# Program order on three engines in the attention of a routing-attention and MLP kernel, and a copy moved from VectorE to ScalarE

## The chip, the cores and the metric

The kernel runs on one core of a Trainium2 chip. The metric is the device time of one execution in microseconds (us). The engines are TensorE (PE in the profile; PEld is its weight load), VectorE (DVE), ScalarE (ACT), GpSimd (POOL) and SyncE (SP), which here issues nearly all DMAs. Each engine works through its own queue, and engines wait for one another by semaphores.

## What is computed

Attention in which a query sees only the keys that fall to the same one of 16 clusters, and then an MLP block with a residual:

```python
q_assign = np.argmax(np.einsum('bhsd,hcd->bhsc', q_n, c_n), axis=-1)   # q_n, k_n, c_n: rows scaled to length 1
k_assign = np.argmax(np.einsum('bhsd,hcd->bhsc', k_n, c_n), axis=-1)
mask = q_assign[:, :, :, None] == k_assign[:, :, None, :]
scores = np.where(mask, scale * np.matmul(q, k.transpose(0, 1, 3, 2)), -1e9)
attn = softmax(scores)                     # written out in the reference, with 1e-9 in the denominator
x = (attn @ v) brought from (B,H,S,D) to (B, S, H*D)
xn = (x - mean(x)) / sqrt(var(x) + 1e-6) * g_ln
out = x + np.maximum(xn @ w_ch1, 0.0) @ w_ch2
```

B = 4, H = 8, S = 768, D = 64; the MLP goes from 512 to 2048 and back. The two weight matrices arrive as 64-bit floats, and the kernel converts them to 32 bits on VectorE.

## The kernel before

The attention runs over 16 head pairs `n` (4 batches by 4 pairs of heads). A pair has 12 steps: two halves of the queries by six blocks of 128 keys. A step is `scores` (four matmuls for two heads: two with the one-hot clusters, L317, two with q and k, L322; then one exponential of 128x768 on ScalarE, L327, into one of five buffers `e`) and `weigh` (the matmuls with v, L337, and on VectorE the addition of the exponentials into `es`, L348 or L351; after the sixth step a ScalarE copy into `xT`, L354).

The loop over `u` has six slots per pair, two steps in each. `scores` runs two steps ahead of `weigh`. Between them stands the preparation of the coming pairs and the end of the pair before:

- slot 0: `prep_transpose(n + 1, 1)`, six PE transposes of k (L230) and two copies out of PSUM, the first half by ScalarE (L236), the second by VectorE (L238);
- slot 1: `prep_sims(n + 1)`, similarities to the centroids (L247) and a ScalarE copy (L256); `finish(n - 1, 0)`, denominators by matmuls with ones (L367), a copy (L372) and four DMAs of it;
- slot 2: `prep_route(n + 1)`, three transposes (L263) and a chain of six VectorE operations (L270 to L282) that gives the one-hot clusters;
- slot 3: `finish(n - 1, 1)`, VectorE's reciprocal (L376) and two kinds of DMA, out to memory and back as a broadcast `rb`;
- slot 4: `prep_onehot(n + 1)`, twelve transposes (L295) and two ScalarE copies (L301);
- slot 5: `prep_transpose(n + 2, 0)`, the same for q; `finish(n - 1, 2)`, VectorE's scaling of `xT` by `rb` (L390).

Two chunks of weights (of 32) are due per pair: `split_weight` in slots 0 and 3 (three VectorE operations, L182 to L188), `join_weight` in slots 1 and 4 (four, L196 to L204), after which `load_weight` fetches the chunk after the next into one of two `raw` buffers. After every fourth chunk of the first matrix (pairs 1, 3, 5 and 7, slot 5) `center_w1` multiplies by a mean matrix on PE (L211) and corrects w1 with four VectorE operations (L215).

The program is written in a tile framework, which places the semaphores itself. Nothing in the kernel before fixes the order of the queues: the framework's planner simulates the engines with its own costs and, on each engine, takes from the instructions that it holds for ready the one that stands earliest in the program. So later work, such as a weight chunk, can go ahead of earlier work that the planner holds for not ready yet. The order is fixed when the program is compiled; the chip runs each queue in it.

The MLP (L470 on) follows with eight rounds of 128 matmuls into `h_ps` (L493) and 96 into `o_ps` (L507).

Of the kernel before, what the change touches and what calls it, by code (L numbers as in the profile page):

```python
# [19 lines left out]
def kernel(  # L20
# [22 lines left out]
    NDC = DM // P  # L43
# [30 lines left out]
    def load(n, names):  # L74
        if n >= len(pairs):
            return
        b, pr = pairs[n]
        for name in names:

            t = loads.tile(  # L80
                [P, NT, 2, D], F32, tag=name, name=f"{name}_sb", bufs=2 if name == "v" else 1
            )
            for j in range(2):
                nc.sync.dma_start(
                    out=t[:, :, j, :],
                    in_={"q": q, "k": k, "v": v}[name][b, 2 * pr + j].rearrange(
                        "(p c) d -> p c d", p=P
                    ),
                )
            loaded[n][name] = t  # L90
# [66 lines left out]
    NW1 = NDC * FF // WC  # L157
# [12 lines left out]
    def load_weight(m):  # L170
        if m < NWC:
            raw = conv.tile([P, WC], mybir.dt.int64, tag="raw", name="raw", bufs=2)
            nc.sync.dma_start(out=raw, in_=weight_chunk(m)[0])
            raws[m] = raw

    def split_weight(m):
        words = raws[m].bitcast(U32).rearrange("p (n w) -> p n w", w=2)
        hi = words[:, :, 1]
        ta = conv.tile([P, WC], U32, tag="ta", name="ta")
        tb = conv.tile([P, WC], U32, tag="tb", name="tb")  # L180

        nc.vector.tensor_scalar(  # L182
            ta, hi, 0x07FFFFFF, 3, op0=ALU.bitwise_and, op1=ALU.logical_shift_left
        )
        nc.vector.scalar_tensor_tensor(  # L185
            out=ta, in0=hi, scalar=0xC0000000, in1=ta, op0=ALU.bitwise_and, op1=ALU.bitwise_or
        )
        nc.vector.tensor_single_scalar(tb, hi, 0x7FF00000, op=ALU.bitwise_and)  # L188
        halves[m] = (ta, tb)
# [33 lines left out]
    def prep_transpose(n, side):  # L223
        src = loaded[n]["qk"[side]]
        t_sb = heads.tile([P, S], F32, tag=f"t{side}", name=f"t{side}")
        prepared[n][side] = t_sb
        for g in range(NHALF):
            t = ps("qk_ps")
            for c in range(TH):
                nc.tensor.transpose(  # L230
                    t[:, c * P : (c + 1) * P],
                    src[:, g * TH + c, :, :].rearrange("p h d -> p (h d)"),
                    ident,
                )
            if g == 0:
                nc.scalar.copy(t_sb[:, g * HC : (g + 1) * HC], t[:, :HC])  # L236
            else:
                nc.vector.tensor_copy(t_sb[:, g * HC : (g + 1) * HC], t[:, :HC])  # L238

    def prep_sims(n):  # L240

        _, pr = pairs[n]
        sim = ps("sim_ps")
        for side in range(2):
            for g in range(NHALF):
                r = (side * NHALF + g) * Q
                nc.tensor.matmul(  # L247
                    sim[r : r + Q, :HC],
                    cT[:, pr, :, :].rearrange("p j c -> p (j c)"),
                    prepared[n][side][:, g * HC : (g + 1) * HC],  # L250
                    start=True,
                    stop=True,
                    tile_position=(0, r),
                )
        sim_sb = route.tile([P, HC], F32, tag="sim", name="sim_sb")
        nc.scalar.copy(sim_sb, sim[:, :HC])  # L256
        prepared[n]["sim"] = sim_sb

    def prep_route(n):
        sim_sb = prepared[n]["sim"]  # L260
        simT = ps("simT_ps")
        for c in range(TH):
            nc.tensor.transpose(  # L263
                simT[:, c * P : (c + 1) * P], sim_sb[:, c * P : (c + 1) * P], ident
            )
        NG = TH * 4 * 2
        sims = simT[:, :HC].rearrange("p (g c) -> p g c", c=NCL)
        revs = rev.unsqueeze(1).to_broadcast([P, NG, NCL])
        best = route.tile([P, NG], F32, tag="best", name="best")
        nc.vector.tensor_reduce(best, sims, AX.X, ALU.max)  # L270
        hit = route.tile([P, NG, NCL], F32, tag="hit", name="hit")
        nc.vector.tensor_tensor(
            hit, sims, best.unsqueeze(2).to_broadcast([P, NG, NCL]), ALU.is_equal
        )

        nc.vector.tensor_tensor(hit, hit, revs, ALU.mult)
        first = route.tile([P, TH, 2, NHALF * 2], F32, tag="first", name="first")
        nc.vector.tensor_reduce(first.rearrange("p c s a -> p (c s a)"), hit, AX.X, ALU.max)
        shape = [P, TH, NHALF * 2, NCL]

        for side, op in ((0, ALU.is_equal), (1, ALU.not_equal)):
            nc.vector.tensor_tensor(  # L282
                onehots[side].rearrange("p c g j d -> p c (g j) d")[:, :, :, :NCL],
                rev.unsqueeze(1).unsqueeze(1).to_broadcast(shape),
                first[:, :, side, :].unsqueeze(3).to_broadcast(shape),
                op,
            )

    def prep_onehot(n):
        for side in range(2):  # L290
            t = ps("oh_ps", BF16, 1024)
            for g in range(NHALF):
                for c in range(TH):
                    o = (g * TH + c) * P
                    nc.tensor.transpose(  # L295
                        t[:, o : o + P],
                        onehots[side][:, c, g, :, :].rearrange("p j d -> p (j d)"),
                        identb,
                    )
            m = heads.tile([P, S], BF16, tag=f"m{side}", name=f"m{side}")  # L300
            nc.scalar.mul(m, t[:, :S], -FAR if side else 1.0)  # L301
            prepared[n]["m", side] = m
# [7 lines left out]
    def scores(i):  # L310
        n, g, c = steps[i]
        st = prepared[n]
        s = ps_s.tile([P, 2, 512], F32, tag="s", name="s_ps")
        keys, cols = slice(c * P, (c + 1) * P), slice(g * HC, (g + 1) * HC)
        rows = [slice(j * D, (j + 1) * D) for j in range(2)]
        for j in range(2):
            nc.tensor.matmul(  # L317
                s[:, j, :HC], st["m", 1][rows[j], keys], st["m", 0][rows[j], cols],
                start=True, stop=False,
            )  # L320
        for j in range(2):
            nc.tensor.matmul(  # L322
                s[:, j, :HC], st[1][rows[j], keys], st[0][rows[j], cols],
                start=False, stop=True,
            )
        e = attn.tile([P, 2, HC], F32, tag="e", name="e", bufs=5)
        nc.scalar.activation(e, s[:, :, :HC], AF.Exp, scale=SCALE)  # L327
        soft[i] = e
# [64 lines left out]
    steps = [(n, g, c) for n in range(len(pairs)) for g in range(NHALF) for c in range(NT)]  # L393
    per = NHALF * NT
    slots = per // 2
    for side in range(2):
        prep_transpose(0, side)
        load(1, "qk"[side])
    prep_sims(0)
    prep_route(0)  # L400
    prep_onehot(0)
    prep_transpose(1, 0)
    load(2, "q")
    load_weight(0)
    load_weight(1)
    scores(0)
    scores(1)
    for u in range(len(pairs) * slots):
        n, slot = divmod(u, slots)
        nxt = n + 1 < len(pairs)  # L410
        if slot == 1:
            load(n + 1, "v")
        if slot == 0 and nxt:
            prep_transpose(n + 1, 1)
            load(n + 2, "k")
        if slot == 1 and nxt:
            prep_sims(n + 1)
        if slot == 2 and nxt:
            prep_route(n + 1)
        if slot == 4 and nxt:  # L420
            prep_onehot(n + 1)
        if slot == 5 and n + 2 < len(pairs):
            prep_transpose(n + 2, 0)
            load(n + 3, "q")
        if slot == 1 and n:
            finish(n - 1, 0)
        for i in (2 * u + 2, 2 * u + 3):
            if i < len(steps):
                scores(i)
        weigh(2 * u)  # L430
        weigh(2 * u + 1)
        if slot == 3 and n:
            finish(n - 1, 1)
        if slot == 5 and n:
            finish(n - 1, 2)
        m = 2 * n + slot // 3
        if slot % 3 == 0:
            split_weight(m)
        elif slot % 3 == 1:
            join_weight(m)  # L440
            load_weight(m + 2)
        elif m < NW1 and m % NDC == NDC - 1:
            center_w1(m // NDC)
    for part in range(3):
        finish(len(pairs) - 1, part)


    def all_in_range():
# [279 lines left out]
```

## Time and profile before

| | |
|---|---|
| median of 3 runs | 1132.69 us (1131.82 to 1133.15) |
| the profiled execution | 1133.01 us |
| its span, from the first to the last instruction | 1131.2 us |
| PE busy | 1076.1 us, 95% |
| VectorE busy | 391.9 us, 35% |
| ScalarE busy | 300.6 us, 27% |
| first matmul of the MLP | 452.55 us |

The attention takes the first two fifths of the span and the MLP the rest. A share of busy time over the whole span is a mean over both, so the views below are of stretches. In a line of a timeline the first number is the start and the second the length in us; `x6` merges six instructions; brackets name the idle time of the engine before the line and what ended it.

### The profile page before, as it was taken

The numbers are of one execution on the slowest core, as the hardware profiler recorded it, in microseconds if no ns is written. First come the engines' busy times: TensorE is split into PE (matmuls) and PEld (weight loads), VectorE is DVE, ScalarE is ACT, GpSimd is POOL, SyncE is SP. The second block draws the span as 40 slices with busy tenths as digits, with TensorE's granted clock in tenths as the row PEclk, the third lists the DMA queues.
The fourth block names the chain that finished last, engine by engine and source line by source line (L and its number), as shares of the span: only waits on it lengthen the run. The fifth ranks groups of instructions, "written<-read, shape, count | busy, mean of one in ns | idle before, by whom it ended". The sixth has DMA issues, their size and how long they took to land.

```text
span 1131.2 us, 11304 instructions
## 1 busy us (share of the span) xinstructions
PE 1076.1 (95%) x4530; PEld 530.5 (47%) x4530; DVE 391.9 (35%) x662; ACT 300.6 (27%) x484; POOL 3.3 (0%) x28
## 2 busy tenths in 40 slices
PE   5897778999999999999999999999999999999997
PEld 3343333444444443554554554554554554554543
DVE  6999999966566565000010010010010010010010
ACT  3443334455655565120110110110110110110110
POOL 1000000000000000000000000000000000000000
PEclk8988989999999999999999999999999999999998
DMA  8444445322223210000000000000000000000000
GB/s 189 119 118 136 130 118 142 83 57 57 71 65 86 62 40 19 14 1 19 9 1 20 8 5 24 1 10 19 1 10 19 1 9 19 1 9 19 1 9 22
DMA packets 91996, 49.28 MB, mean 44 GB/s; under 512 B 82720, under 2 KB 82720, under 8 KB 91936
## 3 DMA queue, kind: packets, MB, share of 16 engines
q1 hardware_dynamic: 91264, 48.45, 15.8%
q8 instruction: 37, 0.61, 0.2%
q14 instruction: 23, 0.19, 0.1%
q10 hardware_dynamic: 672, 0.03, 0.0%
HBM read 41.98 MB, written 6.39 MB: 43 GB/s over the span
## 4 chain that ended last, share of the span: by engine, by line
PE 80%; DVE 14%; DMA 2%; issue 2%; SPq 1%; ACT 0%; DVEq 0%
PE h_ps L493 29%; PE o_ps L507 29%; PE a_ps L337 7%; PE s_ps L322 6%; DVE es L351 3%; PE s_ps L317 2%; DVE tb L201 2%; DVE ta L196 2%; DVE ta L185 1%; PE qk_ps L230 1%; DVE tb L200 1%; PE sim_ps L247 1%; PE x_ps L478 1%; PE den_ps L367 1%; DVE w L204 1%
## 5 line engine op out<-in xcount | busy, mean ns | idle before, releaser
L493 PE MATMUL h_ps<-xT,w 128*128 128x384 f32 x1024 | 331.7, 486 | 0.6 <-ACT dsb L372 0.6
L507 PE MATMUL o_ps<-w,hT 128*128 128x512 f32 x768 | 330.9, 592 | 0.0
L493 PEld LDWEIGHTS h_ps<-xT,w 128*128 128x128 f32 x1024 | 194.7, 190 | 137.9 <-issue 3.3
L507 PEld LDWEIGHTS o_ps<-w,hT 128*128 128x128 f32 x768 | 145.5, 190 | 179.7 <-issue 179.7
L501 ACT ACTIVATE hT<-h_ps 128x384 f32<-128x384 f32 x128 | 62.5, 491 | 542.4 <-PE h_ps L493 531.9
L327 ACT ACTIVATE e<-s_ps 128x768 f32<-128x768 f32 x192 | 152.0, 813 | 77.0 <-PE s_ps L322 77.0
L322 PE MATMUL s_ps<-t,t 64*128 64x384 f32 x768 | 157.3, 488 | 0.0
L337 PE MATMUL a_ps<-e,v_sb 128*64 128x384 f32 x768 | 144.8, 499 | 0.0
L351 DVE TENSOR_TENSOR es<-es,e 128x768 f32<-128x768 f32 x128 | 122.2, 955 | 38.9 <-ACT e L327 33.6
L483 DVE BATCH_NORM_STATS2 bn<-xr 128x6 f32<-128x512 f32 x24 | 15.9, 689 | 323.5 <-ACT xr L481 323.5
L516 DVE SCALAR_TENSOR_TENSOR o_sb<-o_ps,rstd,xr 128x512 f32<-128x512 f32 x24 | 18.0, 751 | 294.9 <-PE o_ps L507 294.9
L337 PEld LDWEIGHTS a_ps<-e,v_sb 128*64 128x64 f32 x768 | 46.7, 136 | 86.9 <-issue 86.8
L322 PEld LDWEIGHTS s_ps<-t,t 64*128 64x128 f32 x768 | 69.9, 192 | 22.1 <-issue 22.1
L317 PE MATMUL s_ps<-m,m 64*128 64x384 bf16 x384 | 64.4, 332 | 0.0
L247 PE MATMUL sim_ps<-t,cT 128*32 128x384 f32 x128 | 21.9, 526 | 28.7 <-DVE t L238 28.7
L317 PEld LDWEIGHTS <-m 64*128 64x128 bf16 x384 | 18.7, 94 | 47.3 <-issue 32.4
L348 DVE TENSOR_TENSOR es<-e 128x768 f32<-128x768 f32 x32 | 30.5, 953 | 14.0 <-ACT e L327 14.0
L301 ACT ACTIVATE m<-oh_ps 128x768 bf16<-128x768 bf16 x32 | 24.2, 808 | 28.1 <-PE oh_ps L295 28.1
L390 DVE TENSOR_TENSOR xT<-xT,rb 128x768 f32<-128x768 f32 x16 | 15.3, 956 | 26.0 <-DMA rb<-row 26.0
L236 ACT COPY t<-qk_ps 128x384 f32<-128x384 f32 x32 | 15.3, 478 | 33.5 <-PE qk_ps L230 33.5
L367 PE MATMUL den_ps<-es,ones 128*32 128x384 f32 x128 | 23.8, 600 | 0.3 <-DVE es L351 0.3
L256 ACT COPY sim_sb<-sim_ps 128x384 f32<-128x384 f32 x16 | 7.6, 478 | 59.9 <-PE sim_ps L247 59.9
(77 smaller groups left out, 411.1 us busy)
## 6 DMA issues: line engine op xcount, KB each, us to landing
raw<-in_moe_w_ch_dram SPq DMA_DIRECT2D x32, 512.0 KB, 3.7
q_sb<-in_q_dram SPq DMA_DIRECT2D x32, 192.0 KB, 3.8
k_sb<-in_k_dram SPq DMA_DIRECT2D x32, 192.0 KB, 4.2
v_sb<-in_v_dram SPq DMA_DIRECT2D x32, 192.0 KB, 3.9
rb<-row SPq DMA_DIRECT2D x32, 192.0 KB, 3.3
out_dram<-o_sb SPq DMA_DIRECT2D x24, 256.0 KB, 2.0
rdens<-dsb SPq DMA_DIRECT2D x64, 1.5 KB, 1.7
row<-rdens SPq DMA_DIRECT2D x16, 6.0 KB, 1.4
```

The lines of the kernel that those rows point to most:

```text
L247: nc.tensor.matmul(sim[r : r + Q, :HC], cT[:, pr, :, :].rearrange("p j c -> p (j c)"), prepared[n][side][:, g * HC : (g + 1) * HC], start= ...
L301: nc.scalar.mul(m, t[:, :S], -FAR if side else 1.0)
L317: nc.tensor.matmul(s[:, j, :HC], st["m", 1][rows[j], keys], st["m", 0][rows[j], cols], start=True, stop=False,)
L322: nc.tensor.matmul(s[:, j, :HC], st[1][rows[j], keys], st[0][rows[j], cols], start=False, stop=True,)
L327: nc.scalar.activation(e, s[:, :, :HC], AF.Exp, scale=SCALE)
L337: nc.tensor.matmul(acc[j * D : (j + 1) * D, :HC], loaded[n]["v"][:, c, j, :], e[:, j, :], start=(c == 0), stop=(c == NT - 1),)
L348: nc.vector.tensor_tensor(es, soft.pop(i - 1), soft.pop(i), ALU.add)
L351: nc.vector.tensor_tensor(es, es, soft.pop(i), ALU.add)
L367: nc.tensor.matmul(den[r : r + Q, :HC], ones, sums[n, g][:, j, :], start=True, stop=True, tile_position=(0, r),)
L493: nc.tensor.matmul(hp[:, :HC], w1[:, c, f * P : (f + 1) * P], xT[b][:, c, r * HC : (r + 1) * HC], start=(c == 0), stop=(c == NDC - 1),)
L501: nc.scalar.activation(hT, hp[:, :HC], AF.Relu)
L507: nc.tensor.matmul(op, hTs[f][:, tt * P : (tt + 1) * P], w2[:, f, :], start=(f == 0), stop=(f == NFC - 1),)
```

## The change

Two things. The copies of the second half of the transposed q and k go from VectorE to ScalarE for every pair but pair 0. And the whole attention, from the first `prep_transpose` to the last `finish`, is traced inside a block that keeps the order of the program text on PE, VectorE and ScalarE. SP's queue, with the DMAs, is not in that set and is still ordered by the planner. The lines of the loop are only indented.

```diff
-            if g == 0:
+            if g == 0 or n:
                 nc.scalar.copy(t_sb[:, g * HC : (g + 1) * HC], t[:, :HC])
             else:
                 nc.vector.tensor_copy(t_sb[:, g * HC : (g + 1) * HC], t[:, :HC])
...
-    for side in range(2):
-        prep_transpose(0, side)
-        load(1, "qk"[side])
-    prep_sims(0)
...
+    order = {mybir.EngineType.PE, mybir.EngineType.DVE, mybir.EngineType.Activation}
+    with tc.manual_schedule(engines=order):
+        for side in range(2):
+            prep_transpose(0, side)
+            load(1, "qk"[side])
+        prep_sims(0)
...
+        for part in range(3):
+            finish(len(pairs) - 1, part)
```

## Rows read from the trace of the kernel before

**Rows 1.** Stretches: length; busy us (instructions) of PE, PEld, DVE, ACT, POOL; clock; DMA.

```profile
150.00:200.00 50.00, 38.39 (x232) 15.77 (x231) 49.11 (x86) 18.42 (x27) 0.00 (x0) 0.90 0.50 140
...
250.00:300.00 50.00, 50.00 (x336) 22.54 (x334) 31.19 (x44) 27.50 (x41) 0.00 (x0) 1.00 0.27 65
```

**Rows 2.** Waits, whole span, PE's and SP's: us in total, times, longest.

```profile
PE sim_ps L247 <- DVE t L238: 28.7, 8, 6.3
...
SPq L173 <- DVE tb L201: 102.6, 27, 7.6
```

**Rows 3.** Timeline, 48 to 60 us: PE and the copy on DVE.

```profile
48.85 0.87 PE L230 MATMUL qk_ps<-ident,k_sb 128*128 128x128 f32 x6
...
52.81 0.85 PE L247 MATMUL sim_ps<-t,cT 128*32 128x384 f32 x6
...
57.28 0.55 DVE L238 COPY t<-qk_ps 128x384 f32<-128x384 f32 x1
...
57.89 0.85 PE L247 MATMUL sim_ps<-t,cT 128*32 128x384 f32 x1 [4.23 <-DVE t L238]
```

**Rows 4.** Timeline of PE: k transposes at starts of pairs 0, 6, 7, 8; mean matmuls.

```profile
23.68 0.88 PE L230 MATMUL qk_ps<-ident,k_sb 128*128 128x128 f32 x6
...
220.15 0.82 PE L230 MATMUL qk_ps<-ident,k_sb 128*128 128x128 f32 x6
...
243.36 0.87 PE L230 MATMUL qk_ps<-ident,k_sb 128*128 128x128 f32 x6
...
266.62 3.70 PE L211 MATMUL mean_ps<-w,mean 128*128 128x512 f32 x8
270.15 0.82 PE L230 MATMUL qk_ps<-ident,k_sb 128*128 128x128 f32 x6
```

**Rows 5.** Groups by line and form: the copies; count, busy us, mean ns, idle before.

```profile
L238 DVE COPY t<-qk_ps 128x384 f32<-128x384 f32 x32 | 17.7, 553 | 4.0 <-PE qk_ps L230 4.0
...
L236 ACT COPY t<-qk_ps 128x384 f32<-128x384 f32 x32 | 15.3, 478 | 33.5 <-PE qk_ps L230 33.5
```

**Rows 6.** Timeline of VectorE: a weight chunk, a centring, the last scaling.

```profile
196.97 0.43 DVE L182 TENSOR_SCALAR ta<-raw 128x512 uint32<-128x512 uint32 x1
...
201.76 0.95 DVE L351 TENSOR_TENSOR es<-es,e 128x768 f32<-128x768 f32 x1
...
220.35 2.72 DVE L215 SCALAR_TENSOR_TENSOR w<-w,g_sb,mean_ps 128x512 f32<-128x512 f32 x4 [0.18 <-PE mean_ps L211]
...
446.05 0.96 DVE L390 TENSOR_TENSOR xT<-xT,rb 128x768 f32<-128x768 f32 x1 [3.16 <-DMA rb<-row]
...
446.92 4.14 DVE L351 TENSOR_TENSOR es<-es,e 128x768 f32<-128x768 f32 x4
```

**Rows 7.** Timeline, 303 to 310 us, VectorE: reciprocal, routing chain, scaling.

```profile
303.93 0.23 DVE L376 RECIPROCAL rdens<-rdens 128x12 f32<-128x12 f32 x1 [1.27 <-DMA rdens<-dsb]
304.07 0.49 DVE L270 TENSOR_REDUCE best<-simT_ps 128x24 f32<-128x384 f32 x1
...
306.92 0.95 DVE L348 TENSOR_TENSOR es<-e 128x768 f32<-128x768 f32 x1
...
309.54 0.96 DVE L390 TENSOR_TENSOR xT<-xT,rb 128x768 f32<-128x768 f32 x1 [1.67 <-DMA rb<-row]
```

**Rows 8.** Timeline, same pair: slot 2's transposes, slot 3's exponentials.

```profile
301.92 0.55 PE L263 MATMUL simT_ps<-ident,sim_sb 128*128 128x128 f32 x3
...
306.59 1.62 ACT L327 ACTIVATE e<-s_ps 128x768 f32<-128x768 f32 x2 [0.44 <-PE s_ps L322]
```

**Rows 9.** Timeline, start-up: similarities, first and last of the routing on VectorE.

```profile
11.94 0.86 PE L247 MATMUL sim_ps<-t,cT 128*32 128x384 f32 x2 [1.93 <-DVE t L238]
...
14.30 0.56 DVE L270 TENSOR_REDUCE best<-simT_ps 128x24 f32<-128x384 f32 x1 [1.09 <-PE simT_ps L263]
...
18.58 0.69 DVE L185 SCALAR_TENSOR_TENSOR ta<-raw,ta 128x512 uint32<-128x512 uint32 x1
```

**Rows 10.** Timeline, the first matmuls of the MLP.

```profile
452.55 3.82 PE L493 MATMUL h_ps<-xT,w 128*128 128x384 f32 x11 [0.59 <-ACT dsb L372]
```

More of the change, by code (lines that the diff above doesn't have):

```diff
@@ L395 @@
     slots = per // 2
-    for side in range(2):
-        prep_transpose(0, side)
-        load(1, "qk"[side])
-    prep_sims(0)
[L400 to L443, printed above, removed]
@@ L444 @@
-    for part in range(3):
-        finish(len(pairs) - 1, part)
+    order = {mybir.EngineType.PE, mybir.EngineType.DVE, mybir.EngineType.Activation}
[4 more added lines that the diff above has]
+        prep_sims(0)
+        prep_route(0)
+        prep_onehot(0)
+        prep_transpose(1, 0)
+        load(2, "q")
+        load_weight(0)
+        load_weight(1)
+        scores(0)
+        scores(1)
+        for u in range(len(pairs) * slots):
+            n, slot = divmod(u, slots)
+            nxt = n + 1 < len(pairs)
+            if slot == 1:
+                load(n + 1, "v")
+            if slot == 0 and nxt:
+                prep_transpose(n + 1, 1)
+                load(n + 2, "k")
+            if slot == 1 and nxt:
+                prep_sims(n + 1)
+            if slot == 2 and nxt:
+                prep_route(n + 1)
+            if slot == 4 and nxt:
+                prep_onehot(n + 1)
+            if slot == 5 and n + 2 < len(pairs):
+                prep_transpose(n + 2, 0)
+                load(n + 3, "q")
+            if slot == 1 and n:
+                finish(n - 1, 0)
+            for i in (2 * u + 2, 2 * u + 3):
+                if i < len(steps):
+                    scores(i)
+            weigh(2 * u)
+            weigh(2 * u + 1)
+            if slot == 3 and n:
+                finish(n - 1, 1)
+            if slot == 5 and n:
+                finish(n - 1, 2)
+            m = 2 * n + slot // 3
+            if slot % 3 == 0:
+                split_weight(m)
+            elif slot % 3 == 1:
+                join_weight(m)
+                load_weight(m + 2)
+            elif m < NW1 and m % NDC == NDC - 1:
+                center_w1(m // NDC)
+        for part in range(3):
+            finish(len(pairs) - 1, part)
```

## The prediction

> **What bounds the kernel now.** I read the table of stretches first. From 150 to 200 us TensorE (PE) is busy 38.4 of 50 us at a granted clock of 0.90, while VectorE is busy 49.1 of 50; from 250 to 300 us PE is busy all 50 at 1.00 and VectorE only 31.2 [rows 1]. So the attention has two halves with two limits: first VectorE, then PE. The code says why. All 32 weight chunks are due over 16 head pairs, but the planner has let VectorE convert them as soon as they land: one of the last runs from 196.97 on [rows 6]. After the attention come eight rounds of the MLP, in which PE has no gaps; the change does not touch them.
>
> Next, what PE waits for in the first half. The totals name one thing: the similarity matmuls (L247) waited 28.7 us, 8 times, for the VectorE copy of the transposed k [rows 2]. One such wait in detail: the six transposes start at 48.85 and take 0.87 us; the copy of their second half runs only at 57.28, and PE, which had begun the similarities at 52.81, stands 4.23 us until 57.89 [rows 3]. The copy did not wait for data. It stood in VectorE's queue behind weight steps that nobody needs for hundreds of microseconds. So the price is one of order on VectorE, not of work.
>
> How fast the stage goes when PE is never late is read from the second half. Pair 7 begins with its k transposes at 243.36 and its mean matmuls start at 266.62: 23.26 us for an ordinary pair. The mean matmuls take until 270.15: 3.53 us more, for pairs 1, 3, 5 and 7 [rows 4]. On PE this half already runs in exactly the order of the program text (I followed slots 0 to 5 of the loop row by row), so the fixed order costs PE nothing there.
>
> **The change part by part.** *PE order.* Same as now, so no cost and no gain of its own. What it takes away is the chance to run something else during a wait, so each wait of PE on another engine now has to be looked at.
>
> *Second copy moved to ScalarE.* For pairs 1 to 15, 30 copies leave VectorE and go to ScalarE. The row next to them is the copy of the first half: 478 ns on ScalarE against 553 ns on VectorE [rows 5]. ScalarE gains some 1 us in 23.26 us, of which it is busy little over half (27.5 of 50 us, rows 1). In slots 0 and 5 it waits for scores anyway after its copies. Cost on the path: between zero and two copies per pair, 0.96 us; I take zero, since the copy that it follows is hidden today.
>
> *VectorE order.* This is the change that counts. Two chunks per pair now run in slots 0, 1, 3 and 4. Does VectorE still fit below PE? Per pair: ten additions of exponentials, 10.35 us if each waits for the one before (four of them in a row took 4.14 us [rows 6]) and 9.5 us at 0.95 each if they overlap; I take 10.35. The routing chain, 304.07 to 306.92, 2.85 us; reciprocal 0.23, final scaling 0.96 [rows 7]. Two chunks: 196.97 to 201.76 holds one chunk and one addition of 0.95, so 3.84 us [rows 6]; in program order one step more stands behind its own input, so I take 4.0, twice. Sum 22.4 us against PE's 23.26: reserve 0.87. With the centring of w1 (four operations, 2.72 us [rows 6]) 25.1 against 26.79. It fits, closely.
>
> Who waits for VectorE inside a pair? First, the exponentials: there are five buffers, so the second one of a slot needs the first addition of the slot before. The tight place is slot 2, where the routing stands ahead of the additions. Slot 2 starts at 301.92 with transposes of 0.55 us; routing until 305.4, the addition until 306.4. The first exponential of slot 3 begins at 306.59 and both take 1.62, so the second begins at 307.4 [rows 8]. Reserve 1.0 us. Second, the one-hot transposes in slot 4, a whole slot after the routing ends. Third, the pair after a centring: centring, three additions and a chunk are 2.72 + 3.1 + 4.0 = 9.8 us after its start; its slot 2 needs the routing from 8.5 + 0.6 = 9.1 on (293.41, that is 270.15 + 23.26, to 301.92). So the routing starts 0.7 us late, inside the reserve of 1.0. Hence I expect PE to run without gaps.
>
> *The new waits of VectorE.* The reciprocal (slot 3) and the final scaling (slot 5) wait for DMAs, and the additions, the centring and the next pair's weight steps are queued behind them. Today the scaling runs 5.61 us after the reciprocal (303.93 to 309.54) and waits for its transfer [rows 7]. In the new order the reciprocal comes at about 308.4 and the scaling after four additions and a chunk, 316.5. The transfer, due at 314.0, is there 2.5 us earlier. Cost zero; if that cover is gone, the delay goes to the next pair, less the reserves above.
>
> *Queues not in the fixed set.* The DMA queue (SP) is still ordered by the planner. Each transfer keeps its place relative to the work that frees its buffer. Bounds: zero, to SP's longest wait for a weight step, 7.6 us [rows 2] (this is the second rival).
>
> *The sum.* Pairs 0 to 5 took from 23.68 to 220.15 = 196.47 us. Without gaps: 6 x 23.26 + 3 x 3.53 = 150.15. Gain 46.3 us. Start-up: PE's wait of 1.93 us for the copy that stood behind a weight step goes, and the first routing, 14.30 to 18.58 = 4.28 us with weight steps mixed in, becomes 2.85: together 3.4 us [rows 9]. End: the additions that waited behind the scaling (3.16 us for its transfer [rows 6]) come before it now, but the last chunk's second half now stands ahead of the last additions, so the MLP, which starts at 452.55 after the denominators [rows 10], gains nothing: 0, between -1.5 and +1.5. Total 49.7. Span 1131.2 - 49.7 = 1081.5; the profiled run took 1.8 us more than its span, which gives 1083.3; it lay 0.3 above the median of the runs, which gives **1083**.
>
> **The rivals.** *A: VectorE becomes the bound.* For it: the reserve of 0.87 us per pair is 4% and stands on durations from another mix; in program order each weight step follows its own input. Against it: I took the longer addition and PE's period from a stretch with the same work. If VectorE needs 8% more, 24.2 us, PE loses 1 us in each of 15 pairs: 1083 + 15 = 1098.
>
> *B, slower: VectorE stands at the final scaling.* SP's queue could put the broadcast transfer behind a weight load that waits for a weight step; SP stood up to 7.6 us that way [rows 2]. PE feels a delay after the 2.5 us of cover and the two reserves, 0.87 and 1.0, so from 4.4 us on; the 49.7 us are used up at 3.3 us per pair over 15 pairs, so from a delay of 7.7 us in every pair. At 10 us it is 15 x 5.6 = 84 us lost: 1167. For it: VectorE waits for that transfer already. Against it: the delay would have to exceed, in each pair, the longest one seen.
> VectorE is shown to keep its order: the scaling at 446.05 waited 3.16 us, and four additions ran in one row right behind it from 446.92 [rows 6]. The Trainium skill says the same in "PSUM — Partial Sum Buffer", section "Engine vs sequencer instructions": "ScalarE/VectorE/GpSimdE queues are strict FIFO." By that rule, which speaks against a fixed order with two DMA waits in it, this rival follows whenever the transfer is late; the trace agrees, and its chance hangs on SP alone.
>
> *C: the order does not bind VectorE's weight steps.* If they still ran as soon as they land, only the moved copies would help: 12 copies of 0.55 us less on a VectorE that bounds the first six pairs, 6.6 us, and the start-up's 1.9 us: 1083 + 49.7 - 8.5 = 1124. Against it: the diff names VectorE.
>
> **How the numbers follow.** The forecast (1078 to 1090) gets 0.75, A 0.13, C 0.05, B 0.05, no difference 0.02. The range goes from 1078 (end +1.5, additions that overlap, the first pair without denominators) to 1098, A's value, and leaves out under 2 in 10. About 0.2% is what a measurement of this kernel can tell from no change. Faster: 0.93; within 0.2%: 0.02; slower: 0.05.
>
> **What would show it.** In the table of stretches, PE busy all the time at clock 1.00 from about 25 us on, VectorE at some 90% up to the end of the attention instead of 98% and then 62%; k transposes every 23.26 or 26.8 us from the first pair; no wait of L247 on a t copy; similarity copies and scores of the first pair some 3.4 us earlier; the MLP's first matmul near 403 us. Wrong would be: PE waiting for one-hots, for exponentials that wait for an addition (A), or VectorE idle before L390 for over 4 us (B).

## The result and the profile after

The changed kernel takes 1081.28 us (median of 4 runs, 1080.80 to 1081.68) against 1132.38 us (4 runs, 1131.82 to 1133.15) for the kernel before on the same chip: a ratio of 0.9548, interval 0.9532 to 0.9565. The profiled execution took 1080.8 us with a span of 1079.0.

First the chain that ended last, by engine, from the page of the kernel before:

```profile
PE 80%; DVE 14%; DMA 2%; issue 2%; SPq 1%; ACT 0%; DVEq 0%
```

Then the page of the kernel after, with its busy times and the same chain:

```profile
span 1079.0 us, 11243 instructions
...
PE 1062.3 (98%) x4530; PEld 527.4 (49%) x4530; DVE 381.6 (35%) x632; ACT 311.9 (29%) x514; POOL 3.3 (0%) x28
...
PE 98%; DMA 0%; DVE 0%; SPq 0%; ACT 0%; issue 0%
```

VectorE's 14% of the chain are gone. Its share of busy time over the span is 35% in both kernels, so this number shows nothing of the change. The stretches do (length; busy us and instructions of PE, PEld, DVE, ACT, POOL; clock; DMA):

```profile
28.30:60.00 31.70, 31.70 (x227) 14.31 (x225) 27.69 (x45) 20.19 (x30) 0.00 (x0) 1.00 0.34 88
...
150.00:200.00 50.00, 50.00 (x338) 22.51 (x336) 43.45 (x68) 29.03 (x45) 0.00 (x0) 1.00 0.41 107
...
250.00:300.00 50.00, 50.00 (x351) 22.54 (x349) 43.03 (x68) 30.41 (x47) 0.00 (x0) 1.00 0.45 116
```

The two halves of the attention are gone. From 150 to 200 us PE was busy 38.39 of 50 us and VectorE 49.11, from 250 to 300 it was 50.00 and 31.19 [rows 1]; now PE is busy all the time in both, and VectorE 43 us in both. The same work is spread over the whole attention: before, the last of the 32 weight chunks was done at 216.9 us, now at 397.6.

What PE waits for, whole span (total, times, longest):

```profile
PE ct_ps L144 <- DVE c_sb L139: 4.7, 1, 4.7
PE oh_ps L295 <- DVE onehot_q L282: 2.8, 1, 2.8
PE h_ps L495 <- ACT dsb L372: 0.6, 1, 0.6
```

The wait of L247 for the t copy, 28.7 us in 8 places [rows 2], is not there any more. What is left belongs to the start and to the step into the MLP.

The pairs, by the k transposes at the starts of pairs 0, 1, 2, 6 and 8, and by the first matmuls of the MLP:

```profile
19.31 0.88 PE L230 MATMUL qk_ps<-ident,k_sb 128*128 128x128 f32 x6
...
42.08 0.87 PE L230 MATMUL qk_ps<-ident,k_sb 128*128 128x128 f32 x6
...
68.87 0.82 PE L230 MATMUL qk_ps<-ident,k_sb 128*128 128x128 f32 x6
...
168.89 0.82 PE L230 MATMUL qk_ps<-ident,k_sb 128*128 128x128 f32 x6
...
218.89 0.82 PE L230 MATMUL qk_ps<-ident,k_sb 128*128 128x128 f32 x6
...
400.98 9.30 PE L495 MATMUL h_ps<-xT,w 128*128 128x384 f32 x28 [0.59 <-ACT dsb L372]
```

From 168.89 to 218.89 two pairs take 50.00 us, which is 23.2 for an ordinary one and 26.8 for one with the mean matmuls. The first six pairs show the same periods as the later ones, but for pair 0, which has no pair before it to finish and takes 22.8 (19.31 to 42.08). The 52.2 us of span saved lie as follows:

| part | before | after | saved | predicted |
|---|---|---|---|---|
| start to the first k transpose | 23.68 | 19.31 | 4.4 | 3.4 |
| pairs 0 to 5 | 196.47 | 149.58 | 46.9 | 46.3 |
| pair 6 to the first matmul of the MLP | 232.40 | 232.09 | 0.3 | 0 |
| MLP to the end | 678.65 | 678.02 | 0.6 | 0 |
| sum | 1131.2 | 1079.0 | 52.2 | 49.7 |

### The profile page after: what moved, and what is told of

Its sections match the earlier page's. It is cut to its first block, busy times and chain, and to the rows that moved or that the text cites. A ratio compares the mean times of both kernels' runs of the same rounds, so it can differ in the third digit from the quotient of the medians.

```text
span 1079.0 us, 11243 instructions
## 1 busy us (share of the span) xinstructions
PE 1062.3 (98%) x4530; PEld 527.4 (49%) x4530; DVE 381.6 (35%) x632; ACT 311.9 (29%) x514; POOL 3.3 (0%) x28
## 4 chain that ended last, share of the span: by engine, by line
PE 98%; DMA 0%; DVE 0%; SPq 0%; ACT 0%; issue 0%
PE h_ps L495 31%; PE o_ps L509 31%; PE a_ps L337 13%; PE s_ps L322 11%; PE s_ps L317 4%; PE qk_ps L230 2%; PE mean_ps L211 1%; PE sim_ps L247 1%; PE oh_ps L295 1%; PE den_ps L367 1%; PE x_ps L480 1%; PE simT_ps L263 1%; DMA k_sb<-in_k_dram 0%; SPq L84 0%; ACT e L327 0%; DVE o_sb L518 0%
## 5 line engine op out<-in xcount | busy, mean ns | idle before, releaser
L322 PE MATMUL s_ps<-t,t 64*128 64x384 f32 x768 | 155.1, 482 | 0.0
L317 PEld LDWEIGHTS <-m 64*128 64x128 bf16 x384 | 18.7, 93 | 44.0 <-issue 28.7
L236 ACT COPY t<-qk_ps 128x384 f32<-128x384 f32 x62 | 26.9, 482 | 32.9 <-PE qk_ps L230 32.9
L201 DVE SCALAR_TENSOR_TENSOR tb<-raw,tb 128x512 f32<-128x512 uint32 x32 | 22.2, 692 | 1.1
L185 DVE SCALAR_TENSOR_TENSOR ta<-raw,ta 128x512 uint32<-128x512 uint32 x32 | 22.2, 692 | 1.1
L204 DVE TENSOR_TENSOR w<-tb,ta 128x512 f32<-128x512 f32 x32 | 22.1, 692 | 1.1
L196 DVE SCALAR_TENSOR_TENSOR ta<-tb,ta 128x512 f32<-128x512 uint32 x32 | 21.9, 684 | 0.0
```

The source lines that it names most:

```text
L185: nc.vector.scalar_tensor_tensor(out=ta, in0=hi, scalar=0xC0000000, in1=ta, op0=ALU.bitwise_and, op1=ALU.bitwise_or)
L317: nc.tensor.matmul(s[:, j, :HC], st["m", 1][rows[j], keys], st["m", 0][rows[j], cols], start=True, stop=False,)
L322: nc.tensor.matmul(s[:, j, :HC], st[1][rows[j], keys], st[0][rows[j], cols], start=False, stop=True,)
```

## Experiments

Theory: what counts is the place of the weight work in VectorE's queue. Spread as the program text has it, VectorE needs less per pair than PE, and PE never waits. Rivals: the moved copies carry a part of the gain (R1); a fixed order as such is what helps, wherever the weight work stands (R2); the fit is so narrow, or the two DMA waits in the fixed order so costly, that a little more would tip it (R3, the prediction's A and B). In the compiled programs, PE's queue and ScalarE's have the same order before and after through the attention, the moved copies aside; VectorE's and SP's differ. A kernel with only VectorE in the fixed set compiles to the same four queues as the kernel after, and one with only PE and ScalarE in it to the same as the copies alone. So of the three fixed orders it is VectorE's that makes the difference, with SP's, which the planner derives beside it; no run parts these two.

### The order without the copies

```diff
-            if g == 0 or n:
+            if g == 0:
```

> The fixed order, but both second copies stay on VectorE for every pair. Theory (VectorE's order is what counts): VectorE gets 30 copies of 0.55 us back, 1.1 us per pair, and in the changed kernel it still stood 1.6 us per ordinary pair before the routing, so TensorE should not wait: 1080 to 1084 us, k transposes every 23.3 us. Rival (the copy's move is what counts): the waits of the similarities for the copy, 28.7 us in the kernel before, come back: about 1110 us.

Measured: 1080.91 us (1080.16 to 1081.67), ratio to the kernel before 0.9537 (0.9522 to 0.9553), against 0.9548 (0.9532 to 0.9565) with both parts. The order alone brings the whole gain. A stretch of it, columns as above:

```profile
150.00:200.00 50.00, 50.00 (x338) 22.52 (x334) 44.95 (x73) 27.51 (x40) 0.00 (x0) 1.00 0.43 107
```

Against the kernel after, VectorE is busy 1.5 us more in this stretch and ScalarE 1.5 us less; either has the idle time for it.

### The copies without the order

The line of the diff on L235 alone, in the kernel before.

> The copies move to ScalarE, the order is left to the planner. Theory: the weight steps still run ahead on VectorE, which bounds the first pairs; only the copies' own time there (12 x 0.55 us) and the start-up wait go: about 1124 us (1116 to 1132), TensorE waiting for the one-hots or the exponentials in place of the copy. Rival (the copy's move is what counts): the 28.7 us of waits for the copy go and nothing takes their place: about 1104 us.

Measured: 1133.81 us (1132.79 to 1135.57), ratio 1.0008 (0.9998 to 1.0018): no difference. The theory had expected about 1124 us (1116 to 1132) and the rival 1104, so both missed. The waits and one place show where it went (PE's waits, a timeline of PE, a timeline of VectorE just before):

```profile
PE oh_ps L295 <- DVE onehot_q L282: 38.6, 7, 7.3
...
PE sim_ps L247 <- DVE t L238: 1.3, 1, 1.3
```

```profile
62.95 1.51 PE L337 MATMUL a_ps<-e,v_sb 128*64 128x384 f32 x8
71.75 0.82 PE L295 MATMUL oh_ps<-identb,onehot_q 128*128 128x128 bf16 x6 [7.29 <-DVE onehot_q L282]
```

```profile
61.50 0.42 DVE L182 TENSOR_SCALAR ta<-raw 128x512 uint32<-128x512 uint32 x1
...
64.80 0.69 DVE L204 TENSOR_TENSOR w<-tb,ta 128x512 f32<-128x512 f32 x1
...
66.95 0.95 DVE L351 TENSOR_TENSOR es<-es,e 128x768 f32<-128x768 f32 x1
67.82 0.55 DVE L270 TENSOR_REDUCE best<-simT_ps 128x24 f32<-128x384 f32 x1
```

The copy is off VectorE and PE no longer waits for it (28.7 us [rows 2], now 1.3), but the next thing that PE needs from the same queue, the routing, stands behind weight chunks: its transposes were done at 58.1, a whole chunk ran from 61.50 (L182) to 65.49 (L204) meanwhile, and the routing's first operation started at 67.82. Before, the one-hots cost PE 10.2 us, here 38.6. R1 falls. Taking one victim out of a queue that holds later work in front moves the wait to the next victim.

### No weight work at all, order free

```diff
+    nc.gpsimd.memset(w1, 0.015625)
+    nc.gpsimd.memset(w2, 0.015625)
...
-    load_weight(0)
-    load_weight(1)
...
-        if slot % 3 == 0:
-            split_weight(m)
-        elif slot % 3 == 1:
-            join_weight(m)
-            load_weight(m + 2)
-        elif m < NW1 and m % NDC == NDC - 1:
+        if slot % 3 == 2 and m < NW1 and m % NDC == NDC - 1:
```

> The kernel before, order free and copies on VectorE, without the loads and the conversion of the weights: both weight matrices are filled with a constant by GpSimd, all other work stays. Theory (the planner's order is harmful only where it puts weight steps ahead): TensorE runs without gaps as in the changed kernel, 1079 to 1085 us. Rival (the planner's order is poor in itself): gaps of TensorE stay, over 1100 us.

Measured: 1093.29 us (1092.89 to 1093.69), ratio 0.9665 (0.9637 to 0.9693). This is above the range expected, and the surplus is the experiment's own. While GpSimd fills the matrices (3.80 to 17.58 us), VectorE's scaling of the centroids, 0.25 us long in the kernel after, lasts 13.23; the first matmul waits for it and starts at 17.78 instead of 4.74. Timelines of VectorE and of PE:

```profile
4.40 13.23 DVE L139 TENSOR_SCALAR c_sb<-c_sb,c_tmp 128x64 f32<-128x64 f32 x1
```

```profile
17.78 0.39 PE L144 MATMUL ct_ps<-ident,c_sb 128*64 128x128 f32 x1 [17.78 <-DVE c_sb L139]
...
413.89 6.39 PE L488 MATMUL h_ps<-xT,w 128*128 128x384 f32 x19 [0.59 <-ACT dsb L374]
```

The start is 13.04 us later than in the kernel after, the MLP 12.91; without that the time would be about 1080, inside the range. Between the two, the planner's free order is as good as the program's order with the weights in it, with PE busy 100.00 of 100 us from 100 to 200 us. So the free order costs nothing where there is no weight work to pull ahead.

### The order fixed, the weight work early

The kernel after with four chunks per pair in pairs 0 to 7 instead of two in all 16.

```diff
-            m = 2 * n + slot // 3
-            if slot % 3 == 0:
+            m = 4 * n + (0, 1, 1, 2, 3, 3)[slot]
+            if slot % 3 != 2 and m < NWC:
                 split_weight(m)
-            elif slot % 3 == 1:
                 join_weight(m)
                 load_weight(m + 2)
-            elif m < NW1 and m % NDC == NDC - 1:
+            elif slot == 5 and m < NW1:
                 center_w1(m // NDC)
```

The two halves of a chunk now stand one behind the other, and the centrings come in pairs 0 to 3.

> The changed kernel with the same fixed order, but the text converts four chunks per pair in pairs 0 to 7 in place of two in all 16. Theory (what counts is when VectorE gets the weight work, not that the order is fixed): VectorE needs 13.2 us of its own work and 4 x 3.85 us of weights, 28.6 us per pair against 23.3 us of TensorE, and 31.3 against 26.8 in the pairs with a centring: 4 x 5.3 + 4 x 4.5 = 39 us lost, 1115 to 1128 us. Rival (fixing the order is what helps): 1081 to 1086 us.

Measured: 1122.27 us (1122.13 to 1122.41), ratio 0.9921 (0.9892 to 0.9950): four fifths of the gain are gone though the order is fixed as before. R2 falls. The stretch looks like the kernel before again:

```profile
150.00:200.00 50.00, 42.23 (x276) 18.98 (x276) 47.83 (x80) 24.33 (x37) 0.00 (x0) 0.97 0.42 107
```

### The order free, the loads held back

Before each load from the third chunk on, GpSimd copies one column of the current pair's sums into the load's buffer, so the load can't start earlier.

```diff
+            if gate is not None:
+                nc.gpsimd.tensor_copy(raw.bitcast(F32)[:, 0:1], gate[:, 0, 0:1])
...
-            load_weight(m + 2)
+            load_weight(m + 2, sums[steps[2 * u + 1][:2]])
```

> The kernel before, order free and copies on VectorE; but each weight load from the third chunk on first waits for a one-column GpSimd copy of the current pair's sum of exponentials into its buffer, so that a chunk can't land before its pair. Theory (the harm is that weight steps stand ahead of the pair's own work on VectorE): VectorE's load is spread over 16 pairs as in the changed kernel, and most of the gain comes without any fixed order: 1081 to 1095 us. Rival (the fixed order itself is needed, whatever the weights do): over 1115 us.

Measured: 1156.71 us (1156.57 to 1158.19), ratio 1.0205 (1.0188 to 1.0222): some 2% slower. The theory missed by over 60 us, and the time lies where the rival had put it. The trace gives another reason than the rival's: VectorE now stands for the loads. Its waits and one place of its timeline:

```profile
DVE ta L184 <- DMA raw<-in_moe_w_ch_dram: 107.4, 31, 4.7
```

```profile
153.15 0.43 DVE L184 TENSOR_SCALAR ta<-raw 128x512 uint32<-128x512 uint32 x1 [4.06 <-DMA raw<-in_moe_w_ch_dram]
153.49 0.95 DVE L353 TENSOR_TENSOR es<-es,e 128x768 f32<-128x768 f32 x1
154.36 0.69 DVE L187 SCALAR_TENSOR_TENSOR ta<-raw,ta 128x512 uint32<-128x512 uint32 x1
154.97 0.95 DVE L353 TENSOR_TENSOR es<-es,e 128x768 f32<-128x768 f32 x1
155.83 0.55 DVE L272 TENSOR_REDUCE best<-simT_ps 128x24 f32<-128x384 f32 x1
```

VectorE stands for the loads 107.4 us in 31 places, with additions and routing behind it. Presumably the planner puts a chunk's first step where, by its own costs, the load has landed, and on the chip it lands later. So spreading the loads did not help here: the first step also has to stand behind its load's real landing. In the kernel after no chunk waits for its load, since the program text leaves five slots between them. (The gate takes 0.4 us of GpSimd per pair, and it also delays the loads themselves; the experiment can't part the two.) So no run shows a free order that keeps the gain with the weight work in it; that the fixed order as such is not enough is shown by the run before.

### How much room VectorE has

The kernel after with extra additions of 128x768 behind the final scaling of every pair, two in one run and four in another.

```diff
+    def burden(count):
+        for _ in range(count):
+            nc.vector.tensor_tensor(spare2, spare, spare, ALU.add)
...
+                burden(4)
```

> The changed kernel with four further VectorE additions of 128x768 per pair, behind the final scaling in slot 5 (about 3.9 us). Theory: in the changed kernel VectorE stood about 1.6 us before the routing of an ordinary pair; what goes beyond it, 2.3 us in each of some 11 pairs without a centring, falls on TensorE, less 1 us of reserve once: about 1081 + 24 = 1105 us (1098 to 1110). The four pairs with a centring take it in their wait of 3.3 us for the mean product. Rival (VectorE's idle share of 13%, 6.5 in 50 us, is all usable): 6.5 us per two pairs against 7.8, a loss of 0.65 us per pair, some 1088 us.

> The kernel after with two extra VectorE additions of 128x768 per pair (some 1.9 us, results unused) behind the final scaling. Theory, that VectorE has a reserve of some 1.6 us in an ordinary pair (21.2 us plus what four additions of 3.9 us cost, 1.7 us per pair, taken from the run with four): 1.9 us is 0.3 us over it in an ordinary pair, more in none: 1081 to 1086 us. Rival, that VectorE has no reserve and each microsecond on it costs one: 15 x 1.9 = 28 us, 1109 us.

Measured: with four 1106.77 us (1106.17 to 1107.37), ratio 0.9784 (0.9756 to 0.9812); with two 1083.45 us (1082.03 to 1083.89), ratio 0.9560 (0.9542 to 0.9578). The timeline of VectorE with four of them shows what they take, 3.85 us to the next start:

```profile
171.69 3.93 DVE L365 TENSOR_TENSOR spare<-spare 128x768 f32<-128x768 f32 x4
175.54 2.71 DVE L215 SCALAR_TENSOR_TENSOR w<-w,g_sb,mean_ps 128x512 f32<-128x512 f32 x4
```

and PE's k transposes have a period of 24.99 us:

```profile
298.64 0.87 PE L230 MATMUL qk_ps<-ident,k_sb 128*128 128x128 f32 x6
...
323.63 0.88 PE L230 MATMUL qk_ps<-ident,k_sb 128*128 128x128 f32 x6
```

The time with four lies inside the expected range, but the sum behind it was another. An ordinary pair cost 1.7 us and not 2.3, so that the 14 pairs from the first to the last k transposes took 14.3 us longer (20.23 to 373.62, against 19.31 to 358.42 in the kernel after); another 9.2 came from there to the MLP (425.37), where TensorE has less to prepare and at the end waits 4.4 us for the last additions.

With two, the 14 pairs from the first to the last k transposes take 338.97 us, against 339.11 in the kernel after: nothing. Its 3.0 us of span come from the start (1.3) and from the last additions, for which the denominators' matmuls wait 1.77 us.

### A later broadcast

The kernel after with four additional trips from memory to memory ahead of the broadcast `rb` (with one in another run), the trips and the broadcast on GpSimd's queue.

```diff
+            for hop in range(4):
+                further = dram.tile([2, S], F32, tag=f"row{hop}", name="further")
+                nc.gpsimd.dma_start(out=further, in_=row)
+                row = further
...
-                nc.sync.dma_start(
+                nc.gpsimd.dma_start(
```

> The changed kernel, but the reciprocals make four further trips from memory to memory before the broadcast, and these transfers and the broadcast are issued by GpSimd's queue, so that SP is not held up. Theory (VectorE stands at the final scaling with all later work behind it): a delay of the broadcast up to about 2.5 us of cover and 1.6 us of reserve per pair and 1 us once costs nothing; beyond it TensorE loses the rest in each ordinary pair, and 3.3 us less in a pair with a centring. At an estimated 2 us per trip, 8 us: 4 us in each of 11 pairs and 1 us in each of 4, 1081 + 48 = 1129 us; at 10 us, 1160 us. Rival (VectorE passes by the waiting scaling): no change, 1081 to 1083 us.

> The kernel after with one additional memory-to-memory trip before the broadcast of the denominators, both on GpSimd's queue. A trip took 2.1 to 4.9 us in the run with four, so the scaling's transfer lands 2 to 5 us later than in the kernel after, of which some 2.5 us lie in the cover between reciprocal and scaling. Theory (VectorE stands at the scaling only for what exceeds the cover, and PE feels it only beyond VectorE's reserve of some 1.6 us and the buffers' 1 us): VectorE waits 0 to 2.5 us at the scaling in each pair, and the time stays within 1080 to 1086 us. Rival, that any wait in the fixed order reaches PE in full: up to 15 x 2.5 = 37 us, some 1100 to 1118 us.

Measured: with four 1211.05 us (1210.21 to 1211.88), ratio 1.0706 (1.0675 to 1.0737), more than the 1129 to 1160 expected, since a trip took 2.0 to 5.8 us and not 2. No run moved the broadcast to GpSimd's queue without a trip, so what that move costs by itself is in these numbers too. VectorE's waits, and one of them with what is behind it:

```profile
DVE xT L394 <- DMA rb<-further: 174.3, 16, 13.6
```

```profile
179.97 0.96 DVE L394 TENSOR_TENSOR xT<-xT,rb 128x768 f32<-128x768 f32 x1 [11.23 <-DMA rb<-further]
180.84 0.95 DVE L348 TENSOR_TENSOR es<-e 128x768 f32<-128x768 f32 x1
...
193.26 0.22 DVE L376 RECIPROCAL rdens<-rdens 128x12 f32<-128x12 f32 x1
```

PE pays at second hand: the additions stand behind the scaling, ScalarE's exponentials wait for their buffers, PE for the exponentials (the same kernel's waits):

```profile
ACT e L327 <- DVE es L348: 108.7, 14, 9.3
...
PE s_ps L317 <- ACT e L327: 65.3, 21, 7.4
```

With one trip 1088.94 us (1084.95 to 1092.74), ratio 0.9600 (0.9575 to 0.9625), 3 us above the range of the theory and 11 under the rival's. In the profiled execution, the slowest of the four, VectorE waited 0.5 to 5.5 us at the scalings of all pairs but the last, 39.1 us together. PE's pairs are no longer than in the kernel after, but for two; those come after waits of 5.49 and 3.93 us and cost 2.1 and 1.7:

```profile
149.40 0.96 DVE L394 TENSOR_TENSOR xT<-xT,rb 128x768 f32<-128x768 f32 x1 [5.49 <-DMA rb<-further]
```

```profile
409.17 1.50 PE L367 MATMUL den_ps<-es,ones 128*32 128x384 f32 x6 [4.41 <-DVE es L351]
```

The second row is the rest: in the last pairs less and then nothing is prepared any more, PE is faster there and VectorE has no room, so what VectorE is behind by then comes out in full: from the last k transposes to the MLP it takes 48.4 us, against 42.6 in the kernel after. With the two longer pairs (3.8), the start (0.8) and what lies behind the MLP's first matmul (1.7) this is the 12.0 us of span that the execution is longer.

### One rule for all of them

The steps of VectorE in a pair of the kernel after, start to start, from its timeline:

```profile
151.23 0.56 DVE L270 TENSOR_REDUCE best<-simT_ps 128x24 f32<-128x384 f32 x1 [1.57 <-PE simT_ps L263]
...
154.14 2.01 DVE L351 TENSOR_TENSOR es<-es,e 128x768 f32<-128x768 f32 x2
156.07 0.95 DVE L348 TENSOR_TENSOR es<-e 128x768 f32<-128x768 f32 x1
156.94 0.22 DVE L376 RECIPROCAL rdens<-rdens 128x12 f32<-128x12 f32 x1
157.07 0.36 DVE L182 TENSOR_SCALAR ta<-raw 128x512 uint32<-128x512 uint32 x1
...
158.42 2.01 DVE L351 TENSOR_TENSOR es<-es,e 128x768 f32<-128x768 f32 x2
160.35 0.68 DVE L196 SCALAR_TENSOR_TENSOR ta<-tb,ta 128x512 f32<-128x512 uint32 x1
...
162.86 2.02 DVE L351 TENSOR_TENSOR es<-es,e 128x768 f32<-128x768 f32 x2
164.79 0.95 DVE L390 TENSOR_TENSOR xT<-xT,rb 128x768 f32<-128x768 f32 x1
169.09 2.72 DVE L215 SCALAR_TENSOR_TENSOR w<-w,g_sb,mean_ps 128x512 f32<-128x512 f32 x4 [3.34 <-PE mean_ps L211]
```

Ten additions are 4 x 1.93 + 2 x 0.87 = 9.46 us, two chunks 2 x (1.35 + 2.51) = 7.72, routing 2.91, reciprocal 0.13, scaling 0.87: 21.1. An ordinary pair then takes the longer of PE's 23.26 and VectorE's 21.1 plus what is added to it:

| kernel | added to VectorE per pair | VectorE | measured, ordinary pair |
|---|---|---|---|
| after | 0 | 21.1 | 23.26 |
| two additions | 1.86 (313.37 to 315.23) | 23.0 | 23.26 |
| four additions | 3.85 (171.69 to 175.54) | 24.95 | 24.99 |
| four chunks instead of two | 7.72 | 28.8 | 28.9 (mean of pairs 4 to 7, 26.4 to 30.6) |
| four trips | 11.23 of waiting | 32.3 | 32.5 (160.76 to 193.26) |

In the last row the wait is measured in the same pair, so it shows only that VectorE has no other gap there; the rows above it add up work alone. So R3 does not hold: beyond the 2.1 us to spare a round grows by the excess alone (four additions: 3.85 - 2.1 = 1.7 us), and one trip more before the broadcast costs 7.7 of the 51.1 us gained.

## Why the prediction was right

It said 1083 (1078 to 1098), and 1081.28 came out. By its own steps:

- *What bounds.* Right. Two halves with two limits, and a price of order and not of work: the run without weights and the one with the weights early show both sides of it.
- *PE order: no cost, no gain.* Right: the queue of PE is the same in both kernels.
- *Second copies: zero on the path.* Right, 1080.91 without them. What the prediction gave them on their own (6.6 us and part of the start-up, in rival C) was wrong: measured alone they bring nothing. It had taken VectorE's first half as bound by a sum of work; freed time there goes to the next chunk, and PE's wait to the next operation in the queue.
- *Pairs 0 to 5, 46.3 us.* 46.9: pair 0 took 22.8 and not 23.26, since it has no denominators to finish.
- *VectorE per pair, 22.4 us and a reserve of 0.87.* Too high: 21.1, reserve 2.1. Mis-sized were the additions, 10.35 where 9.46 came (the overlapping end, 9.5, of its bounds), and the chunks, 8.0 where it is 7.72. The choice was on the cautious side and made rival A likelier than it was: A needed VectorE 8% over 22.4, and it came out 6% under.
- *After a centring.* Right: the routing of pair 7 starts at 178.45, 0.5 us after its transposes (predicted 0.7 late), and ScalarE never waits for an exponential buffer.
- *Cover of the scaling.* Right: the scaling comes 7.85 us after the reciprocal (156.94 to 164.79), predicted 8.1; its transfer is issued at 158.60 and such a one takes 3.1 to 4.4 us. It waits for its transfer in the last pair alone (4.7 us, after the MLP has begun).
- *SP's queue.* Right at the low end of its bounds: no wait of SP reached VectorE. But the upper bound was too low: SP's loads stood behind weight steps 48.9 us in 19 places, and the longest wait was 11.5 us, not 7.6.
- *Start-up.* 4.4 instead of 3.4. The wait of 1.93 us [rows 9] goes and the routing is short, as said; beside that the first q transposes started 0.5 us earlier, at 5.43, since their load came earlier, and the stretch from the one-hots to the k transposes shrank by 0.75 us. It is the clock: from 14 to 28.3 us the granted clock was 0.69 and is now 0.88, a mean of stretches at 1.2 and 2.4 GHz, with PE busy 10.1 us there before and 13.4 now. The first four score matmuls of pair 0 in the timelines of PE, before and after:

```profile
21.42 1.49 PE L322 MATMUL s_ps<-t,t 64*128 64x384 f32 x4
```

```profile
17.77 0.81 PE L322 MATMUL s_ps<-t,t 64*128 64x384 f32 x4
```

- *End: nothing.* 0.3 to the MLP and 0.6 behind it, inside the ±1.5. The last additions do stand behind the last chunk's second half (join 394.96, additions 397.48), as said.
- *Rival B.* Not what happened, but its mechanism is real: four trips give it in full. VectorE stood 11.2 us at the scaling and an addition ran right behind it. "ScalarE/VectorE/GpSimdE queues are strict FIFO", in the Trainium skill's "PSUM — Partial Sum Buffer", section "Engine vs sequencer instructions"; the trace agrees, with 174.3 us of such waits. Its threshold was somewhat low: a delay was to be felt from 2.5 + 1.9 us on, so from a wait of 1.9 us; with one trip, a wait of 2.50 us behind an ordinary pair passed without a longer pair, one of 3.93 cost 1.7 and one of 5.49 cost 2.1. (Waits of up to 4.87 us passed where a centring follows, since VectorE waits up to 3.3 us for the mean product there anyway.) The wait less its cost is 3.4 us in the one pair and 2.3 in the other, which came behind the wait of 2.50; VectorE's reserve of 2.1 and the buffers' 1.0 make 3.1. Its price per pair was right in form: the wait less the reserve.

What was argued and not shown: why the planner holds the earlier work for not ready. The runs show that the weight work is what it pulls ahead, and that with held loads VectorE stands for them; its own costs were not looked at.

## What to carry to other kernels

Read busy shares by stretch: an engine at 35% of the span can be the bound of a fifth of it, when work that is due later is done there early. Before you fix an order, add up what each engine needs per round from start to start, and the waits that the order puts into it; it fits as long as this sum stays under the bounding engine's round, and beyond that each microsecond costs about one, as the table above has it. At the end of the stage, where the bounding engine has less to do, look again: what the other one is behind by then comes out there. Moving a late operation to another engine helps little while the work in front of it stays where it is: the wait goes to the next one in the queue.

## What was not expected of the hardware

- VectorE additions that don't depend on each other overlap at their ends and dependent ones don't: an addition of 0.95 us that doesn't need the one before it is followed 0.87 us after its start, and two that add to the same sums take 1.93 from the first start to what follows. Four that write one tile and read none of each other's results lie between, 0.99 us from start to start (3.93 us for the four at 171.69). Over ten additions this is 0.9 us against the dependent row that the prediction used [rows 6].
- Four trips of 6 KB from memory to memory in a chain, issued by GpSimd, had 2.0 to 5.8 us from one issue to the next (163.47, 165.51, 167.65, 172.53, 176.04 us in one pair). The spread is wider than the shortest trip, and it goes with the other traffic: from 163.5 to 167.6 us, with the DMA engines busy 0.11, two trips took 2.0 and 2.1 us; from 167.7 to 176, with SP's loads running and a busy share of 0.82, the next two took 4.9 and 3.5. In the pair after it is the same, 2.0 and 2.2 us at 0.07 and 4.5 and 4.0 at 0.86. With one trip VectorE's waits ran from 0.5 to 5.5 us, and the kernel's times from 1084.95 to 1092.74, where those of the kernel after stay within 0.9 us.
- While GpSimd filled the weight matrices, two small VectorE operations of 0.25 and 0.22 us lasted 13.23 and 13.13, until the fills were done (L139 and L97, from 4.40 and 4.57 us on, in the run without weight work). The run doesn't show what held them.
